# Pinning PSUM banks in an attention and two-layer MoE kernel: one bank for the first products of block 2, three for its attention

## The chip, the cores and the metric

The kernel runs on one NeuronCore of one Trainium2 chip. The metric is the device time of one execution in microseconds (us), the median of several. TensorE (PE) multiplies matrices and writes its results to PSUM, which has eight banks of 128 partitions by 2 KB. ScalarE (ACT) and VectorE (DVE) read them out of there, GpSimd (POOL) helps with element-wise work between tiles in SBUF, and SyncE (SP) issues most transfers.

## The reference

Three stages follow each other; the output of each is the input of the next.

```python
# q, k, v: (4, 8, 576, 64); omega: (128, 64)
def phi(x):                       # x already scaled by 64 ** -0.25
    h = x @ omega.T - sum(x * x, -1) / 2
    return exp(h - max(h, -1)) / sqrt(128)
q_p, k_p = phi(q_s), phi(k_s)
kv, z = k_p.T @ v, sum(k_p, axis=seq)
x = (q_p @ kv) / (q_p @ z + 1e-06)        # -> 2304 tokens x 512
h = x @ w_in                               # layer 1: 512 -> 2048
x = (h * clip(h + 3, 0, 6) / 6) @ w_out    # 2048 -> 512
h = x @ w_in2                              # layer 2: 512 -> 2048
x = (h * sigmoid(1.702 * h)) @ w_out2      # 2048 -> 512
```

## The kernel before, in words

**Stages.** The 4 x 576 = 2304 tokens are cut into four blocks of 512 (n = 0 to 3, one per batch) and a left-over block of 4 x 64 = 256 (i = B = 4). The attention of block 0 runs alone at the start (the head). Then layer one runs block by block. While layer one works on block n, the attention steps of block n + 1 are issued between its matmuls (`side()` takes them from the list `todo`), so block 2 carries the attention of block 3, the last one, and block 3 has no attention beside it but computes the left-over block as well. Layer two follows with a scheme of seven half-size products.

**Layer one** has 16 chunks c of 128 hidden columns per block. `emit_h` makes the first product of a chunk, `ps` (12 matmuls of 128x512, line 489: four pieces of the inner dimension, each as three products of a high and a low part). ACT applies relu (line 500), DVE the upper limit and the factor (line 501); only then is the bank of `ps` free. ACT and DVE split the result into two parts `gs` (lines 505, 506). `emit_o`, two chunks later (LAG = 2), multiplies `gs` with the second weights into `o` (line 531, 12 matmuls), which stays in its banks over all 16 chunks. In block 3 each chunk has these products twice, at 512 and at 256 columns.

**Attention steps** on PE are the projection with omega (line 265: pieces of 64 rows by 128), transposes of the features (line 345), k-features times v (lines 323, 331), q-features times that (lines 362, 371), and transposes of the normalised result (line 409, and 418 for the left-over rows). Their results leave PSUM through DVE (maximum, line 271; normalisation, lines 389, 393, 397) and ACT (exp, line 273; copy of `kv`, line 339; high part of x, line 255). Meanwhile ACT, DVE and POOL also prepare the weights of layer two (lines 189 to 229).

**PSUM.** Two pools of four banks. `acc` holds `o`. `psp` has one tag "ps" with four interchangeable banks: each request, from `emit_h` or from an attention step through `bank()`, takes whichever bank comes free.

```python
    acc = ctx.enter_context(tc.tile_pool(name="acc", bufs=4, space=PSUM))
    psp = ctx.enter_context(tc.tile_pool(name="psp", bufs=4, space=PSUM))
```

In block 3 the left-over block's `o` takes two banks of `psp` for the whole block. Layer two uses both pools.

**Order.** No order is written out by hand: a scheduler orders each engine's instructions by a timeline of its own, in which the banks that are free take part. So a change of the pools moves instructions on PE, ACT and DVE in all stages, also where the code of a stage is not touched. At run time each engine keeps its order.

Of the kernel before, what the change touches and what calls it, by code (L numbers as in the profile page):

```python
# [8 lines left out]
F32 = mybir.dt.float32  # L9
# [8 lines left out]
PSUM = bass.MemoryType.PSUM  # L18
# [4 lines left out]
def performer_moe_kernel(  # L23
# [18 lines left out]
    B, NPAIR, P = qk.shape[:3]  # L42
# [27 lines left out]
    wp = wctx.enter_context(tc.tile_pool(name="wp", bufs=1))  # L70
    dp = ctx.enter_context(tc.tile_pool(name="dp", bufs=1, space=DRAM))
    acc = ctx.enter_context(tc.tile_pool(name="acc", bufs=4, space=PSUM))
    psp = ctx.enter_context(tc.tile_pool(name="psp", bufs=4, space=PSUM))
    actx = ExitStack()
    at = actx.enter_context(tc.tile_pool(name="at", bufs=1, side="right"))

# [7 lines left out]
    banks = ["both"]  # L84

    def bank(shape, name):
        n_ps[0] += 1
        if banks[0] == "acc" or banks[0] == "both" and n_ps[0] % 2:
            return acc.tile(shape, F32, tag="acc", name="acc")
        return psp.tile(shape, F32, tag="ps", name="ps")  # L90

    def behind(*ins):
        stack = ExitStack()
# [386 lines left out]
    def emit_h(n, c, side):  # L480
        w = ws[0, "i", c].rearrange("p s (k f) -> p s k f", k=NK)
        for i, N in SEGS[n]:
            pool = lp if i == B else gp
            x = xblk[i]
            ps = psp.tile([P, N], F32, tag="ps", name="ps")
            m = 0
            for kk in range(NK):
                for wi, xi in ((0, 0), (0, 1), (1, 0)):
                    nc.tensor.matmul(  # L489
                        out=ps,  # L490
                        lhsT=w[:, wi, kk, :],
                        rhs=x[:, xi, kk, :],
                        start=(m == 0),
                        stop=(m == 3 * NK - 1),
                    )
                    m += 1
                if kk == 1:
                    side()
            g = pool.tile([P, N], F32, tag="ga", bufs=3, name="ga")
            nc.scalar.activation(out=g, in_=ps, func=AF.Relu, bias=three)  # L500
            nc.vector.scalar_tensor_tensor(  # L501
                out=g, in0=g, scalar=6.0, in1=ps, op0=ALU.min, op1=ALU.mult
            )
            s = pool.tile([P, 2, N], F32R, tag="gs", bufs=3, name="gs")
            gate[0] = nc.scalar.copy(s[:, 0, :], g)  # L505
            gate[1] = nc.vector.tensor_tensor(  # L506
                out=s[:, 1, :], in0=g, in1=s[:, 0, :].bitcast(F32), op=ALU.subtract
            )
            if i == n:
                late_at("next")  # L510
                late_at("gate")
            hgt[i, c] = s
            side()
# [3 lines left out]
    def emit_o(n, c, side):  # L517
        for i, N in SEGS[n]:
            w = ws[0, "o", c]
            s = hgt.pop((i, c))  # L520
            per = SM // N
            num = NK // per
            if c == 0:
                pool, tag = (psp, "ps") if i == B else (acc, "acc")
                oacc[i] = [pool.tile([P, per, SM // per], F32, tag=tag, name="o") for _ in range(num)]
            for d, ps in enumerate(oacc[i]):
                for e in range(per):
                    j = d * per + e
                    cols = slice(j * P, (j + 1) * P)
                    for m, (wi, gi) in enumerate(((0, 0), (1, 0), (0, 1))):  # L530
                        nc.tensor.matmul(  # L531
                            out=ps[:, e, :],
                            lhsT=w[:, wi, cols],
                            rhs=s[:, gi, :],
                            start=(c == 0 and m == 0 and e == 0),
                            stop=(c == NC - 1 and m == 2 and e == per - 1),
                            skip_group_check=per > 1,
                        )
                if c == NC - 1:
                    ob = evict(ps.rearrange("p e s -> p (e s)"), 1.0 / 6.0, n == B - 1)  # L540
                    nc.sync.dma_start(
                        out=xs[i][d * per:(d + 1) * per].rearrange("e p s -> p e s"),
                        in_=ob.rearrange("p (e s) -> p e s", e=per),
                    )
                if d == 1:
                    side()
            side()
# [112 lines left out]
    ps = bank([P, 4, P], "ps")  # L660
# [122 lines left out]
    for u in range(len(units) + LAG):  # L783
        while fetches and fetches[0][0] <= u + AHEAD:
            fetch_w(0, *fetches.pop(0)[1:])
        if u < len(units):
            n, c = units[u]
            if c == 0 and n + 1 < B:
                xblk[n + 1] = new_x(n + 1)
                steps = att_steps(Att(n + 1, xblk[n + 1], xl))  # L790
                todo = steps[::-1]
                pace[:] = len(todo), 0, 8 * (n > 0)
            if (n, c) == (B - 2, NC - 1):
                while todo:
                    todo.pop()()
                actx.close()
                lp = ctx.enter_context(
                    tc.tile_pool(name="lp", bufs=1, side="right", reuse_waits="tile")
                )
                xblk[B] = new_x(B)  # L800
                for kk in range(NK):
                    split_x(xl, xblk[B], kk)
            if n > 0:
                before_chunk(n, c)
            emit_h(n, c, side)
            if n == 0:
                convert_next(2, min(c + 2, NC), *(att.feat[H - 1] if c == 0 else ()))
            if (n, c) == (B - 1, PREP):
                assert n_late[0] == len(late)
                prep, _ = x_ops(0, wp, "w")  # L810
            if c == NC - 1:
                while todo:
                    todo.pop()()
        if u >= LAG:
            emit_o(*units[u - LAG], side)
# [5 lines left out]

    def h_pair(p, u, side, first_split):

        psum, tag, oth, otag = (acc, "acc", psp, "ps") if u % 2 else (psp, "ps", acc, "acc")
        w = {}

        def product(op, kind, j, ps, first):
# [88 lines left out]
        if last:  # L916
            rest(1, pl)
            if u % 2 == 0:
                pool, tag = ((l1, "xr"), (xp_, "xl"), (l1, "gl"), (l1, "xr"))[u // 2]
# [28 lines left out]
    def o_pair(p, side):  # L948
# [75 lines left out]
        def banks(pool, tag):  # L1024
            return [pool.tile([P, 2, H2], F32, tag=tag, name="o") for _ in range(2)]
# [15 lines left out]
        def left_bank(pool, tag):  # L1041
            return pool.tile([P, 2, H2], F32, tag=tag, name="o") if last else [None, None]
# [8 lines left out]
        if last:  # L1051
            tl = lp.tile([P, 4, H2], F32, tag="xo0", name="ob")
            tm = lp.tile([P, 4, H2], F32, tag="xo1", name="ob")
        l17 = left_bank(psp, "ps")
        o1 = banks(psp, "ps")
        product(1, o1, True, l17[:, 0] if last else None)
        if last:
            nc.scalar.copy(tl[:, 0], l17[:, 0])
# [4 lines left out]
        product(7, o7, True, l17[:, 1] if last else None)  # L1063
        if last:
            nc.scalar.copy(tl[:, 1], l17[:, 1])
        l6 = left_bank(psp, "ps")
        o6 = banks(acc, "acc")
        product(6, o6, True, l6[:, 0] if last else None)
        if last:
            add(tl[:, 2], tl[:, 0], l6[:, 0])  # L1070
        for j in range(2):
            add(u2[j], u2[j], o6[j])
        o5 = banks(psp, "ps")
        l5 = left_bank(acc, "acc")
        product(5, o5, True, l5[:, 0] if last else None)
        for j in range(2):
# [136 lines left out]
```

## Time and profile before

| | |
|---|---|
| median of 3 runs | 916.0 us (914.94 to 916.13) |
| the profiled execution's own time | 914.51 us |
| its span in the profile | 912.7 us, granted clock 0.998 |
| PE busy in the span | 896.9 us (98%) |
| DVE, ACT, POOL busy | 556.0, 477.4, 322.7 us |

The span runs from the first to the last instruction of the profile; 1.8 us of the execution lie around it. In the span, the head lasts to about 57 us, layer one's blocks 0 to 3 to about 173, 289, 410 and 548 us, and layer two to the end.

### The profile page before, as it was taken

The numbers are of one execution on the slowest core, as the hardware profiler recorded it, in microseconds if no ns is written. First come the engines' busy times: TensorE is split into PE (matmuls) and PEld (weight loads), VectorE is DVE, ScalarE is ACT, GpSimd is POOL, SyncE is SP. The second block draws the span as 40 slices with busy tenths as digits, with TensorE's granted clock in tenths as the row PEclk, the third lists the DMA queues.
The fourth block names the chain that finished last, engine by engine and source line by source line (L and its number), as shares of the span: only waits on it lengthen the run. The fifth ranks groups of instructions, "written<-read, shape, count | busy, mean of one in ns | idle before, by whom it ended". The sixth has DMA issues, their size and how long they took to land.

```text
span 912.7 us, 16524 instructions
## 1 busy us (share of the span) xinstructions
PE 896.9 (98%) x6344; PEld 764.8 (84%) x6344; DVE 556.0 (61%) x952; ACT 477.4 (52%) x973; POOL 322.7 (35%) x257
## 2 busy tenths in 40 slices
PE   8899999999999999999999999999999999999998
PEld 6677777788788788878888888778999888899998
DVE  5887787473744745558553343777876433367784
ACT  6888776376654765656542333444544232244442
POOL 0122222054736656374772112974000244330000
PEclk9999999999999999999999999999999999999999
DMA  7677678688888987778765436999889555465562
GB/s 227 224 252 271 216 268 299 250 308 269 306 284 296 351 303 291 251 268 288 278 227 188 152 121 234 369 398 307 274 293 326 204 165 181 161 174 152 141 199 78
DMA packets 74415, 224.57 MB, mean 246 GB/s; under 512 B 7520, under 2 KB 13792, under 8 KB 74336
## 3 DMA queue, kind: packets, MB, share of 16 engines
q1 hardware_dynamic: 73872, 223.12, 71.1%
q8 instruction: 50, 0.82, 0.4%
q10 hardware_dynamic: 464, 0.39, 0.1%
q14 instruction: 29, 0.24, 0.1%
HBM read 160.57 MB, written 62.91 MB: 245 GB/s over the span
## 4 chain that ended last, share of the span: by engine, by line
PE 84%; DVE 7%; ACT 6%; issue 1%; POOL 1%; DMA 0%; DVEq 0%; SPq 0%; ACTq 0%
PE o L976 20%; PE o L531 19%; PE ps L489 19%; PE h L832 15%; PE ps L265 3%; PE hl L849 2%; ACT e L273 2%; PE ps L362 1%; PE ps L323 1%; DVE w L212 1%; PE ps L345 1%; DVE mx L271 1%; ACT wtop L189 1%; DVE gs L506 1%; DVE wtop L197 1%
## 5 line engine op out<-in xcount | busy, mean ns | idle before, releaser
L489 PE MATMUL ps<-x,wss 128*128 128x512 f32 x768 | 194.6, 398 | 1.5 <-ACT wss L215 0.7
L976 PE MATMUL o<-wss,gs 128*128 128x256 f32 x1512 | 182.1, 283 | 0.1
L976 PEld LDWEIGHTS o<-wss,gs 128*128 128x128 f32 x1512 | 181.6, 191 | 0.8 <-DVE gs L945 0.5
L489 PEld LDWEIGHTS ps<-x,wss 128*128 128x128 f32 x768 | 140.4, 189 | 33.7 <-ACT wss L215 2.4
L832 PE MATMUL h<-xo,wss 128*128 128x512 f32 x672 | 160.2, 394 | 0.9 <-DVE t L865 0.9
L832 PEld LDWEIGHTS h<-xo,wss 128*128 128x128 f32 x672 | 124.1, 188 | 28.7 <-DVE t L865 1.7
L204 POOL TENSOR_TENSOR w<-w,wpow 128x1024 f32<-128x1024 f32 x32 | 69.3, 2164 | 202.9 <-DVE wpow L201 150.8
L501 DVE SCALAR_TENSOR_TENSOR ga<-ga,ps 128x512 f32<-128x512 f32 x80 | 50.1, 631 | 121.9 <-ACT ga L500 121.9
L873 POOL TENSOR_TENSOR g<-g,c 128x512 f32<-128x512 f32 x48 | 64.1, 1337 | 168.4 <-ACT g L872 168.1
L944 ACT CAST gs<-g 128x512 fp32r<-128x512 f32 x112 | 69.4, 621 | 87.1 <-PE o L976 80.7
L531 PE MATMUL o<-gs,wsh 128*128 128x512 f32 (+1 forms) x480 | 112.3, 378 | 1.2 <-ACT gs L505 1.0
L531 PE MATMUL o<-gs,wss 128*128 128x512 f32 (+1 forms) x480 | 109.9, 374 | 0.1
L229 POOL TENSOR_TENSOR wsn<-w,wsn 128x512 fp32r<-128x512 f32 x64 | 86.6, 1368 | 62.3 <-ACT wsn L228 58.2
L945 DVE TENSOR_TENSOR gs<-g,gs 128x512 fp32r<-128x512 f32 x112 | 79.9, 716 | 40.6 <-ACT gs L944 39.0
L531 PEld LDWEIGHTS o<-gs,wsh 128*128 128x128 f32 x480 | 82.2, 188 | 19.0 <-ACT gs L505 1.3
L500 ACT ACTIVATE ga<-ps,three 128x512 f32<-128x512 f32 x80 | 51.4, 650 | 89.2 <-PE ps L489 88.9
L531 PEld LDWEIGHTS o<-gs,wss 128*128 128x128 f32 x480 | 82.4, 188 | 16.2 <-ACT gs L505 0.3
L506 DVE TENSOR_TENSOR gs<-ga,gs 128x512 fp32r<-128x512 f32 x80 | 62.8, 795 | 16.6 <-ACT gs L505 14.7
L273 ACT ACTIVATE e<-ps,mx 128x128 f32<-128x128 f32 x220 | 60.9, 394 | 21.9 <-DVE mx L271 21.9
L872 ACT ACTIVATE g<-c 128x512 f32<-128x512 f32 x48 | 30.3, 632 | 61.5 <-DVE c L865 61.5
L505 ACT CAST gs<-ga 128x512 fp32r<-128x512 f32 x80 | 45.9, 579 | 27.5 <-DVE ga L501 27.1
L228 ACT CAST wsn<-w 128x512 fp32r<-128x512 f32 x64 | 38.2, 620 | 38.4 <-DVE w L212 13.3
(132 smaller groups left out, 1101.4 us busy)
## 6 DMA issues: line engine op xcount, KB each, us to landing
wss<-left SPq DMA_DIRECT2D x56, 512.0 KB, 3.8
wss<-ws0i SPq DMA_DIRECT2D x48, 512.0 KB, 4.7
wraw<-in_w_in_dram SPq DMA_DIRECT2D x32, 512.0 KB, 5.0
wraw<-in_w_out_dram SPq DMA_DIRECT2D x32, 512.0 KB, 6.2
left<-wsn SPq DMA_DIRECT2D x32, 512.0 KB, 3.9
wss<-ws0o SPq DMA_DIRECT2D x24, 512.0 KB, 4.7
ws0i<-wss SPq DMA_DIRECT2D x16, 512.0 KB, 3.1
wss<-sumsa SPq DMA_DIRECT2D x16, 512.0 KB, 3.8
```

The source lines that it names most:

```text
L204: nc.gpsimd.tensor_tensor(out=w, in0=w, in1=q, op=ALU.mult)
L229: nc.gpsimd.tensor_tensor(out=s[:, :, 1], in0=t, in1=s[:, :, 0].bitcast(F32), op=ALU.subtract)
L273: act = nc.scalar.activation(out=e[:, r, :], in_=ps[:, r, :], func=AF.Exp, bias=mx[:, r:r + 1])
L489: nc.tensor.matmul(out=ps, lhsT=w[:, wi, kk, :], rhs=x[:, xi, kk, :], start=(m == 0), stop=(m == 3 * NK - 1),)
L500: nc.scalar.activation(out=g, in_=ps, func=AF.Relu, bias=three)
L506: gate[1] = nc.vector.tensor_tensor(out=s[:, 1, :], in0=g, in1=s[:, 0, :].bitcast(F32), op=ALU.subtract)
L531: nc.tensor.matmul(out=ps[:, e, :], lhsT=w[:, wi, cols], rhs=s[:, gi, :], start=(c == 0 and m == 0 and e == 0), stop=(c == NC - 1 and m == ...
L832: nc.tensor.matmul(out=ps, lhsT=s[:, wi, q, :], rhs=xop[q, op][:, xi], start=(first and m == 0), stop=(m == 5), skip_group_check=not first,)
L873: mul = eng.tensor_tensor(out=g, in0=g, in1=src, op=ALU.mult)
L944: split_ins[0] = nc.scalar.copy(hi, g)
L945: split_ins[1] = nc.vector.tensor_tensor(out=lo, in0=g, in1=hi.bitcast(F32), op=ALU.subtract)
L976: last_row[0] = nc.tensor.matmul(out=out, lhsT=s[:, gi, d * P:(d + 1) * P], rhs=w[:, wi, :], start=(start and m == 0), stop=(stop and m == 2),
```

## The change

The pool `psp` is cut into two tags: "pa" with three banks and "ph" with one. A small class gives them out. In block 2 (`SPLIT[0]`, set for n == 2) the first products of layer one use "ph" alone and the attention steps "pa" alone. Everywhere else a request takes, in turn, pa, pa, pa, ph, by a count of the requests, so a request's tag is settled when the program is written, whichever bank is free. In block 3 the left-over block's `o` lies in two of the three "pa" banks; the products there take turns over the other "pa" bank (three of four) and "ph". In layer two the tags are written out, and the count starts anew at each pair.

```diff
-    psp = ctx.enter_context(tc.tile_pool(name="psp", bufs=4, space=PSUM))
+    pspp = ctx.enter_context(tc.tile_pool(name="psp", bufs=1, space=PSUM))
+
+    class Turns:
+
+        n = 0
+
+        def tile(self, shape, dtype, tag, name):
+            if tag == "ps":
+                Turns.n += 1
+                tag = "pa" if Turns.n % 4 else "ph"
+            return pspp.tile(shape, dtype, tag=tag, bufs=3 if tag == "pa" else 1, name=name)
+
+    psp = Turns()
+    SPLIT = [False]
...
-        return psp.tile(shape, F32, tag="ps", name="ps")
+        return psp.tile(shape, F32, tag="pa" if SPLIT[0] else "ps", name="ps")
...
-            ps = psp.tile([P, N], F32, tag="ps", name="ps")
+            ps = psp.tile([P, N], F32, tag="ps" if not SPLIT[0] else "ph" if i < B else "pa", name="ps")
...
-                pool, tag = (psp, "ps") if i == B else (acc, "acc")
+                pool, tag = (psp, "pa") if i == B else (acc, "acc")
...
             n, c = units[u]
+            SPLIT[0] = n == 2
...
-        psum, tag, oth, otag = (acc, "acc", psp, "ps") if u % 2 else (psp, "ps", acc, "acc")
+        psum, tag, oth, otag = (acc, "acc", psp, "pa") if u % 2 else (psp, "ps", acc, "acc")
+        Turns.n = 0
...
-        l17 = left_bank(psp, "ps")
-        o1 = banks(psp, "ps")
+        l17 = left_bank(psp, "ph")
+        o1 = banks(psp, "pa")
...
-        l6 = left_bank(psp, "ps")
+        l6 = left_bank(psp, "ph")
...
-        o5 = banks(psp, "ps")
+        o5 = [psp.tile([P, 2, H2], F32, tag=tag, name="o") for tag in ("pa", "ph")]
```

The added lines shift the later ones: lines 265, 323, 331, 345, 362, 371, 409, 418, 489 and 531 of before are lines 278, 336, 344, 358, 375, 384, 422, 431, 502 and 544 of the changed kernel.

**PE at the end of block 2's attention.** `x_3514` is block 3's input, `x_2194` block 2's. Before, in PE's order:

```order
L323 MATMUL ps<-v,e 64x65 x8
L331 MATMUL ps<-lv_94,el 64x65 x2
L531 MATMUL o<-gs,wss 128x512 x12
L362 MATMUL ps<-kv,qpt 64x65 x8
L371 MATMUL ps<-kv,qtl 64x65 x2
L531 MATMUL o<-gs,wss 128x512 x12
L409 MATMUL ps<-ident,xt 128x128 x4
L418 MATMUL ps<-ident,xln 64x64 x8
L489 MATMUL ps<-x_2194,wss 128x512 x12
L489 MATMUL ps<-x_3514,wss 128x512 x12
```

In the changed kernel, at the same place:

```order
L544 MATMUL o<-gs,wsh 128x512 x8
L336 MATMUL ps<-v,e 64x65 x8
L344 MATMUL ps<-lv_94,el 64x65 x2
L375 MATMUL ps<-kv,qpt 64x65 x8
L384 MATMUL ps<-kv,qtl 64x65 x2
L422 MATMUL ps<-ident,xt 128x128 x4
L431 MATMUL ps<-ident,xln 64x64 x8
L502 MATMUL ps<-x_3514,wss 128x512 x22
```

The last four attention steps, which had twelve matmuls of layer one between them twice, now follow each other directly, and block 2's last first product no longer stands behind them.

**PE at the start of block 2.** With the numbers of the tiles: `ps_3515`, `ps_3558` are the first products of chunks 0 and 1 of block 2, `ps_3656`, `ps_3657`, `ps_3728` belong to the attention. Before:

```order
L489 MATMUL ps_3515<-x2_2194,wss_3356 128x512 x9
L531 MATMUL o_2346<-gs_3378,wss_3354 128x512
L489 MATMUL ps_3558<-x2_2194,wss_3450 128x512 x9
L531 MATMUL o_2343<-gs_3472,wsh_2071 128x512
L489 MATMUL ps_3515<-x2_2194,wss_3356 128x512
L489 MATMUL ps_3558<-x2_2194,wss_3450 128x512
L531 MATMUL o_2343<-gs_3472,wsh_2071 128x512 x2
L489 MATMUL ps_3515<-x2_2194,wss_3356 128x512 x2
L489 MATMUL ps_3558<-x2_2194,wss_3450 128x512 x2
```

In the changed kernel, from the last part of chunk 0's product to chunk 1's:

```order
L502 MATMUL ps_3515<-x2_2194,wss_3356 128x512 x2
L278 MATMUL ps_3656<-omt_168,qk_3166 128x128
L278 MATMUL ps_3657<-omt_168,qk_3166 128x128
L278 MATMUL ps_3656<-omt_168,qk_3166 128x128
L278 MATMUL ps_3657<-omt_168,qk_3166 128x128
L278 MATMUL ps_3656<-omt_168,qk_3166 128x128
L278 MATMUL ps_3657<-omt_168,qk_3166 128x128
L278 MATMUL ps_3656<-omt_168,qk_3166 128x128
L278 MATMUL ps_3728<-omt_168,lqk_3170 128x128
L502 MATMUL ps_3558<-x2_2194,wss_3450 128x512 x12
```

Both products were open at once, in two banks; now the second starts only behind one group of projection matmuls, in the one bank that the first has used. Over the whole of block 2, stretches of small matmuls (lines 278, 336, 344, 375, 384, 431) in PE's order number 25, against 20 before; over block 1 19 and 19, over block 0 33 against 35.

**PE in block 3.** `x_3514` marks the products of 512 columns, `xl_4805` those of 256. Before, a piece of the middle of the block:

```order
L489 MATMUL ps<-x_3514,wss 128x512 x12
L489 MATMUL ps<-xl_4805,wss 128x256 x12
L531 MATMUL o<-gs,wsh 128x512 x12
L531 MATMUL o<-gs,wsh 128x256 x12
L489 MATMUL ps<-x_3514,wss 128x512 x12
L489 MATMUL ps<-xl_4805,wss 128x256 x12
```

In the changed kernel:

```order
L502 MATMUL ps<-x_3514,wss 128x512 x12
L544 MATMUL o<-gs,wsh 128x256 x2
L544 MATMUL o<-gs,wss 128x512 x12
L544 MATMUL o<-gs,wss 128x256 x12
L502 MATMUL ps<-xl_4805,wss 128x256 x3
L502 MATMUL ps<-x_3514,wss 128x512 x12
L502 MATMUL ps<-xl_4805,wss 128x256 x9
L544 MATMUL o<-gs,wsh 128x512 x12
```

The two first products of a chunk stood side by side; now they mostly have second products between them.

## Rows read from the trace of the kernel before

**Rows 1.** Busy time by engine in two stages: start to end, length, engines, clock, DMA.

```profile
0.00:57.00 57.00, 48.68 (x582) 37.68 (x582) 42.29 (x98) 41.35 (x115) 8.16 (x12) 0.97 0.71 234
...
289.00:410.00 121.00, 120.46 (x910) 96.13 (x907) 68.72 (x113) 74.88 (x169) 70.51 (x63) 1.00 0.83 294
```

**Rows 2.** PE's waits over the whole span: total, times, longest.

```profile
PE acc L362 <- ACT kv L339: 3.0, 3, 1.5
...
PE ps L409 <- DVE den L389: 1.1, 1, 1.1
```

**Rows 3.** PE's waits in block 2, from 289 to 410.

```profile
PE ps L489 <- ACT el L273: 0.4, 1, 0.4
```

**Rows 4.** The chain that ended last, in block 3: start, length, work.

```profile
451.55 4.17 PE o L531 x24
455.72 4.17 PE ps L489 x24
```

**Rows 5.** Timeline of PE around a long stretch of projections: start, length, work.

```profile
308.30 0.86 PE L531 MATMUL o<-gs,wsh 128*128 128x512 f32 x3
309.09 1.16 PE L265 MATMUL ps<-omt,lqk 64*128 64x128 f32 x16
310.18 1.42 PE L531 MATMUL o<-gs,wss 128*128 128x512 f32 x5
```

**Rows 6.** Timeline of PE around a short stretch of projections.

```profile
96.64 0.48 PE L265 MATMUL ps<-omt,qk 64*128 64x128 f32 x2
97.06 1.66 PE L531 MATMUL o<-gs,wsh 128*128 128x512 f32 x6
```

**Rows 7.** Timeline of PE at the end of block 2's attention.

```profile
399.85 3.04 PE L531 MATMUL o<-gs,wss 128*128 128x512 f32 x12
402.82 0.69 PE L362 MATMUL ps<-kv,qpt 128*64 128x65 f32 x16
403.33 0.29 PE L371 MATMUL ps<-kv,qtl 128*64 128x65 f32 x4
403.55 3.04 PE L531 MATMUL o<-gs,wss 128*128 128x512 f32 x12
406.42 0.60 PE L409 MATMUL ps<-ident,xt 128*128 128x128 f32 x4
```

**Rows 8.** Timeline of ACT, then DVE, at that place.

```profile
399.97 0.21 ACT L339 COPY kv<-ps 128x65 f32<-128x65 f32 x1 [0.52 <-PE ps L331]
...
403.67 0.17 DVE L389 TENSOR_SCALAR den<-ps 128x5 f32<-128x5 f32 x1 [2.12 <-PE ps L371]
...
404.09 0.42 DVE L397 TENSOR_TENSOR xt<-ps,rden 128x256 f32<-128x256 f32 x1
```

**Rows 9.** Timeline: one first product and the two reads that free its bank.

```profile
282.70 3.03 PE L489 MATMUL ps<-x,wss 128*128 128x512 f32 x12
...
285.76 0.69 ACT L500 ACTIVATE ga<-ps,three 128x512 f32<-128x512 f32 x1 [0.49 <-PE ps L489]
286.49 0.69 DVE L501 SCALAR_TENSOR_TENSOR ga<-ga,ps 128x512 f32<-128x512 f32 x1 [2.69 <-ACT ga L500]
```

**Rows 10.** Timeline of a first product in block 2 and what frees its bank.

```profile
303.98 2.89 PE L489 MATMUL ps<-x,wss 128*128 128x512 f32 x12
...
309.76 3.58 DVE L212 TENSOR_TENSOR w<-w,wtop 128x512 f32<-128x512 f32 x4
...
313.26 0.67 DVE L501 SCALAR_TENSOR_TENSOR ga<-ga,ps 128x512 f32<-128x512 f32 x1
```

**Rows 11.** Busy time in two slices of the head, columns as in group 1.

```profile
41.00:42.00 1.00, 0.39 (x12) 0.39 (x14) 1.00 (x3) 1.00 (x4) 0.81 (x1) 1.00 0.31 94
...
43.00:44.00 1.00, 1.00 (x17) 0.88 (x18) 0.63 (x2) 1.00 (x5) 0.33 (x1) 0.50 0.99 381
```

**Rows 12.** Timeline of a chunk's 512-column first product early in block 3, and its last read.

```profile
447.22 2.91 PE L489 MATMUL ps<-x,wss 128*128 128x512 f32 x12
...
454.63 1.01 DVE L501 SCALAR_TENSOR_TENSOR ga<-ga,ps 128x512 f32<-128x512 f32 x2
```

## The prediction

> **What bounds the kernel now.** I read the busy time by stage first. PE is busy 896.9 of 912.7 us, and in block 2, where the bank of its own is given, 120.46 of 121.00 us [rows 1]. The list of PE's waits for that block has one entry, 0.4 us, for an exp that empties an attention bank [rows 3]. So next to no wait for a bank is there to be removed in block 2: at most 0.5 us. What PE still has idle lies mostly in the head, 57.00 - 48.68 = 8.3 us of it [rows 1], of which 3.0 us wait for ACT's copy of `kv` and 1.1 us for the normalisation [rows 2]. There DVE and ACT are the busier: 1.00 us each in the slice where PE has 0.39 [rows 11]. The head's PE pauses also show in the clock: a slice right after that one has a granted clock of 0.50, half speed [rows 11].
>
> With PE busy everywhere, time is decided by how long PE's own stream takes: the matmuls at their bare rate, plus what each turn to another shape adds, plus new waits that a changed order opens. The bare rate is in the chain: 24 second products, then 24 first ones of block 3, each time 12 at 512 and 12 at 256 columns, take 4.17 us [rows 4]. With a 256-column matmul at half a 512-column one plus little, that is 0.231 us for 512 columns and 0.117 for 256.
>
> **What a turn to small matmuls costs.** The number of matmuls doesn't change; only into how many stretches the small ones are cut. Around a long stretch of 16 projections, three 512-column matmuls start at 308.30 and the projections at 309.09: 0.79 us, 0.10 more than 3 x 0.231. From the projections' start to the next large one are 1.09 us [rows 5]. A stretch of 2 takes 0.42 us by the same count [rows 6]. So one projection more costs (1.09 - 0.42) / 14 = 0.048 us; a stretch without any would take 0.42 - 2 x 0.048 = 0.32 us, and with the 0.10 of its entry its fixed part is **0.42 us**. That is what one stretch more costs; I let it go from 0.3 to 0.5. Block 2 has five stretches more: 5 x 0.42 = +2.1 us. Block 0 has two fewer: -0.8 us. Block 1 has as many as before. Sum **+1.3 us**, with bounds 0 (the extra stretches lie in waits that PE would have had anyway) and +2.5.
>
> **The end of block 2's attention.** Now twelve second products stand between the k-features' product and the q-features', and twelve more ahead of the transposes [rows 7]. They hide two reads. The copy of `kv` ends at 399.97 + 0.21 = 400.18, and PE was free for its reader at 399.85: 0.33 us, 0.4 with the hand-over. The normalisation ends at 404.09 + 0.42 = 404.51, and PE was free at 403.55: 0.96 us [rows 7, 8]; in the head, where nothing stands between them, PE waits 1.1 us for it [rows 2]. In the changed order the four steps touch, and both reads become waits: 0.4 + 1.1 = **+1.5 us**. Bounds: 0.9 (ACT and DVE come sooner because less stands in their queues) and 4 (an eviction or a weight conversion stands ahead of the copy; the conversion's four DVE instructions take 3.58 us [rows 10]). The transposes' own evictions stay covered by nine matmuls of block 3's first product, 2.1 us. What is late next is nothing: the 24 large matmuls that were cover are executed elsewhere in the block.
>
> **The start of block 2.** A first product's bank is free when DVE has read it: started at 282.70, its matmuls need 12 x 0.231 = 2.77 us, to 285.47, and DVE ends at 286.49 + 0.69 = 287.18, so 1.7 us later when neither engine is held up [rows 9]. In the changed order chunk 1's product follows chunk 0's in the same bank with one stretch of 16 projections between (the order's eight rows of pairs), 1.2 us [rows 5]. PE waits 1.7 - 1.2 = 0.5 us. Chunk 3's product waits about 0.65 us for exp and weight conversions in ACT's queue, by the same comparison, in place of the 0.4 us that chunk 2's attention costs now [rows 3]: +0.25. Together **+0.75 us**, bounds 0 and 5.5 (below). Behind such a wait on PE stand the second products, which are not urgent, and the projections, on whose maximum and exp DVE and ACT then run later.
>
> A rule of the Trainium skill speaks against this part of the change. What the row shows is that a freed bank comes 1.7 us after its matmuls [rows 9]. The page "Perfetto Trace Analysis", section "Optimizing Tensor Performance", says that independent groups of matmuls should go round several PSUM banks, so that the evacuation of one lies beside the next group's matmuls. By it, each of the 16 first products of block 2 would expose its 1.7 us, 27 us in all, and the time would be about 919.1 + 27 - 0.75 = 945. The order speaks against it, since second products and attention lie between most of them, and I give it 0.01, inside rival D.
>
> **The head and the other blocks.** Outside block 2 a request no longer takes the bank that is free first but the one that its turn names. By counting PE's time between two uses of a bank in the new order against 1.7 us, blocks 0 and 1 come to 0 (-0.4 to +0.8). In the head some projections now stand where PE waited for the normalisation, up to 1.1 us [rows 2]; since ACT and DVE are full there, I take half: **-0.5 us** (0 to -1.1). Block 3 has two banks for its first products in place of two interchangeable ones, and three of four fall on one. In its middle that bank always has at least one set of twelve large matmuls, 2.77 us, between two uses, against 1.7 us: **0** (to +8, below). Layer two's banks are the same in number and nothing there waits for `psp`: 0.
>
> **Sum.** 1.3 + 1.5 + 0.75 - 0.5 = +3.1 us. The profiled execution took 914.51 us, 1.5 under the median of 916.0; 914.5 + 3.1 = 917.6, on the median's scale **919.1 us**, +0.34%. A difference under 0.2% (1.8 us; 914.2 to 917.8) can't be told from none.
>
> **Rivals.** A, the forecast, 917.8 to 922: 0.43.
>
> B, no change, about 916.5: the extra stretches and the end's waits fall together. An instruction that waits at the end's reads or at the bank has its shape change behind the wait, and projections that are issued in a wait cost nothing. Then only 1.5 + 0.75 - 0.5 less what the pieces hide remain, or the pieces alone. For it: block 2's DVE and ACT are only 57% and 62% busy [rows 1], so evictions can be prompt. Against it: five stretches can't all lie in 2.25 us of waits that sit at two places. 0.26.
>
> C, faster, about 913.6: the head is reordered as a whole, and PE's idle time there shrinks. 8.3 us are idle [rows 1], 4.1 of them the waits for `kv` and the normalisation [rows 2], and without the longest pause the stretch at half speed, at least 1.0 us of loss in the two slices, would go too [rows 11]. It must give 3.6 + 1.8 = 5.4 us, all of that at once, to pass the mark; at 6 us the time is 919.1 + 0.5 - 6 = 913.6. Or the pieces and the end cost nothing and the head alone gives 2.3. Against it: where PE waits, DVE and ACT are full, and no work is taken from them. 0.19.
>
> D, much slower, over 922, about 926: late releases. In block 2 a product that ended at 306.75 had its bank freed at 313.26 + 0.67 = 313.93, 7.2 us later, because ACT's exps and DVE's 3.58 us of conversion stood ahead [rows 10]. With four banks nobody noticed. With one, a chunk of 121 / 16 = 7.6 us leaves 7.6 - 2.77 = 4.8 us between two first products; beyond 4.8 us each such release costs the difference, here 2.4 us. In block 3 one product, done at 449.99, was freed at 454.63 + 0.69 = 455.3, 5.3 us later [rows 12]; with 3.3 us of cover in the new order early in that block it costs 2.0. Two of each give +8.8 us less what lies in A: 926. Against it: the new order has DVE and ACT in another sequence, which was made with the one bank in view. 0.12.
>
> **How the numbers follow.** Slower by over 0.2%: A and D, 0.55. Within: B, 0.26. Faster: 0.19. The forecast's own range is 917.8 to 922. For 8 in 10 the range reaches down past B into C, to 913.3, and up into D, to 923.5; about 0.11 of C and 0.07 of D lie outside.
>
> **What would show it.** Block 2 longer by about 4 us, with PE's waits listing `kv` and the normalisation at its end (0.4 and 1.1 us) and first products waiting for DVE's read, the minimum and product of line 501 before, at its start; 25 stretches of small matmuls there; blocks 0, 1, 3 and layer two each within 1 us of before; the head shorter by about half a us. I am wrong if block 2 shows no new waits, if the head or layer two moves by more than 2 us, or if block 3's first products wait for their bank.

## The result and the profile after

The changed kernel takes 921.59 us (median of 4, 919.86 to 922.71), the kernel before 915.99: ratio 1.0062, 95% interval 1.005 to 1.0073. It is slower by 5.6 us where 3.1 were forecast; the time lies in the range given and in that of the forecast, 917.8 to 922. The profiled execution took 922.71 us, 8.2 more than that of before. It is the longest of the four, and that of before is 1.5 us under its median, so the sums by stage below are larger than the 5.6 us of the medians.

The same two stages that [rows 1] show, by the same clock times, and a slice early in block 3:

```profile
0.00:57.00 57.00, 47.44 (x586) 36.73 (x587) 42.57 (x100) 41.74 (x115) 8.15 (x12) 1.00 0.75 239
289.00:410.00 121.00, 119.93 (x829) 94.67 (x827) 68.90 (x107) 74.51 (x165) 71.60 (x61) 1.00 0.85 301
418.00:420.00 2.00, 2.00 (x5) 1.61 (x6) 0.69 (x1) 1.70 (x5) 1.10 (x2) 0.50 0.05 15
```

PE is as busy as it was, but in 289 to 410 it got through 829 matmuls where [rows 1] show 910: 76 small ones of the attention, which was over at 407.6 before, now come later, up to 418. And from 418 to 420 its granted clock is 0.50, the lower of its two levels (1.2 of 2.4 GHz). Before, the whole of that stretch ran at 1.00.

Where the time went is seen best when both executions are compared at equal work. For this I weighed every matmul of PE at its bare rate (0.231 us for 512 columns, 0.119 for 256, 0.06 for 128, 0.035 for the narrow ones) and took the difference of the times at which both had done the same sum. By stages, in us against before, with a second profile of the same kernel (experiment e10):

```
stage (before's clock time)            forecast   922.71 run   920.67 run
start to block 2 (to 285)                -1.3        -0.6         -0.2
block 2, body (285 to 399)               +2.0        +2.4         +2.2
end of its attention (399 to 422)        +2.3        +4.5         +2.5
rest of block 3 (422 to 554)              0          +1.0         +1.0
first part of layer two (554 to 657)      0          +1.0         +0.6
sum                                      +3.0        +8.2         +6.2
```

(The forecast's five stretches of small matmuls stand here with three in the body and two at the end, as the trace counts them.) From 657 us on, nothing changes.

In the first stage the head is 0.9 and 0.4 us shorter at 57 us, about as forecast, and block 1 0.8. But block 0, forecast 0.8 shorter, is 1.1 us longer in both runs. First products there wait for weights that ACT prepares (line 228): 2.5 us in three waits from 57 to 173, the longest 1.4 us at 160, where before it was 0.7 us in two.

PE's waits from 289 to 330, and then from 412 to 480:

```profile
PE ps L502 <- DVE ga L514: 1.0, 2, 0.6
```

```profile
PE ps L422 <- DVE xln L410: 1.9, 1, 1.9
PE ps L502 <- DVE ga L514: 1.2, 1, 1.2
PE ps L375 <- ACT kv L352: 0.3, 1, 0.3
```

In [rows 3] block 2 had one wait of 0.4 us. Now the first products of chunks 1 and 3 wait 0.4 and 0.6 us for their one bank; then come the copy of `kv` (line 352), the normalisation (line 410) and one first product in block 3. The end of block 2's attention, PE and then DVE, answering to [rows 7, 8]:

```profile
413.37 0.29 PE L344 MATMUL ps<-lv,el 128*64 128x65 f32 x4
413.97 0.69 PE L375 MATMUL ps<-kv,qpt 128*64 128x65 f32 x16 [0.31 <-ACT kv L352]
414.49 0.29 PE L384 MATMUL ps<-kv,qtl 128*64 128x65 f32 x4
416.71 0.63 PE L422 MATMUL ps<-ident,xt 128*128 128x128 f32 x4 [1.94 <-DVE xln L410]
...
417.91 6.39 PE L502 MATMUL ps<-x,wss 128*128 128x512 f32 x20
```

```profile
411.48 0.42 DVE L410 TENSOR_TENSOR xt<-ps,rden 128x256 f32<-128x256 f32 x1
415.12 0.69 DVE L574 TENSOR_SCALAR ob<-o 128x512 f32<-128x512 f32 x1 [3.22 <-DMA xs<-ob]
415.73 0.15 DVE L402 TENSOR_SCALAR den<-ps 128x5 f32<-128x5 f32 x1
415.92 0.19 DVE L406 RECIPROCAL rden<-den 128x5 f32<-128x5 f32 x1
416.14 0.42 DVE L410 TENSOR_TENSOR xt<-ps,rden 128x256 f32<-128x256 f32 x1
416.48 0.21 DVE L410 TENSOR_TENSOR xln<-ps,rden 128x64 f32<-128x64 f32 x1
```

Two things are to be seen. First, the four steps touch, as the order said, and PE pauses twice. Second, the pause ahead of the last transposes isn't the normalisation's own length. PE is through with its input at 414.8, but DVE begins at 415.73: ahead of it in DVE's queue stands an eviction of block 2's output (line 574), which has stood idle 3.22 us for a store that must free its buffer `ob`. Before, the attention ended ahead of block 2's output, so that no such eviction was there. And then the twenty large matmuls from 417.91, which at the bare rate take 20 x 0.231 = 4.6 us, take 6.4.

### The profile page after: what moved, and what is told of

It reads as the page before. It is cut to its first block, busy times and chain, and to the rows that moved or that the text cites. A ratio compares the mean times of both kernels' runs of the same rounds, so it can differ in the third digit from the quotient of the medians.

```text
span 920.9 us, 16509 instructions
## 1 busy us (share of the span) xinstructions
PE 898.3 (98%) x6344; PEld 764.7 (83%) x6344; DVE 557.9 (61%) x952; ACT 478.2 (52%) x973; POOL 321.4 (35%) x257
## 4 chain that ended last, share of the span: by engine, by line
PE 76%; DVE 6%; ACT 6%; DMA 5%; POOL 5%; issue 3%; SPq 0%; DVEq 0%; POOLq 0%; ACTq 0%
PE o L991 19%; PE ps L502 17%; PE o L544 17%; PE h L847 12%; PE ps L278 3%; PE hl L864 2%; DMA xr<-xs 2%; ACT e L286 2%; PE ps L375 1%; DMA xs<-ob 1%; DMA qk<-in_qk_dram 1%; POOL wsn L242 1%; PE ps L336 1%; PE ps L358 1%; ACT wtop L202 1%
## 5 line engine op out<-in xcount | busy, mean ns | idle before, releaser
L514 DVE SCALAR_TENSOR_TENSOR ga<-ga,ps 128x512 f32<-128x512 f32 (+1 forms) x80 | 49.9, 633 | 124.6 <-ACT ga L513 124.3
L513 ACT ACTIVATE ga<-ps,three 128x512 f32<-128x512 f32 (+1 forms) x80 | 51.0, 651 | 96.5 <-PE ps L502 96.2
L519 DVE TENSOR_TENSOR gs<-ga,gs 128x512 fp32r<-128x512 f32 (+1 forms) x80 | 64.0, 805 | 25.8 <-ACT gs L518 24.5
L518 ACT CAST gs<-ga 128x512 fp32r<-128x512 f32 (+1 forms) x80 | 46.1, 579 | 39.0 <-DVE ga L514 38.3
L225 DVE TENSOR_TENSOR w<-w,wtop 128x512 f32<-128x512 f32 x64 | 47.5, 789 | 14.2 <-POOL w L217 14.2
```

Source lines behind the costliest of these rows:

```text
L519: gate[1] = nc.vector.tensor_tensor(out=s[:, 1, :], in0=g, in1=s[:, 0, :].bitcast(F32), op=ALU.subtract)
```

## The experiments

Theory A, held from here on: the split makes the loss in block 2, most of it at the end of the attention. Its rivals: pinned banks outside block 2 (B), the single bank and the cut stretches all over the body (B2), the dependency alone without DVE's queue (C). The letters of the experiments are these, not those of the prediction's cases.

**e1: pinned banks, no split.**

```diff
-            SPLIT[0] = n == 2
+            SPLIT[0] = False
```

> The changed kernel with block 2 not split: there too the requests take pa, pa, pa, ph in turn. In the order of PE the last normalisation of block 2's attention has 12 first and 9 second products behind it again before its transposes. Theory A (the loss is made in block 2 by the bank of its own and lies mostly at the end of its attention, where PE pauses and then runs at half clock): no half-clock stretch at the start of block 3, the shift there below 1.5 us; what is left is about -0.6 from the head, +1.2 from the shared bank of block 3 and +0.8 at the start of layer two, so 916 to 918.5. Rival B (the loss comes from pinned banks outside block 2, where before any free bank would do): 920.5 to 922.5, as the changed kernel.

919.05 us (6 runs), ratio 1.0044 (1.0029 to 1.006): half a microsecond above A's range, lower than B's. The end of block 2 costs 0.1 us here, as A had it, and the profiled run shows another loss, 7.9 us in the body of block 2. That run, 923.06, is the longest of the six; the other five took 918.5 to 919.7, so they can't have had all of it. DVE, PE, and the clock there:

```profile
311.95 3.57 DVE L225 TENSOR_TENSOR w<-w,wtop 128x512 f32<-128x512 f32 x4
315.45 0.67 DVE L514 SCALAR_TENSOR_TENSOR ga<-ga,ps 128x512 f32<-128x512 f32 x1
```

```profile
316.18 1.16 PE L278 MATMUL ps<-omt,qk 64*128 64x128 f32 x16 [1.49 <-DVE ga L514]
318.44 5.49 PE L502 MATMUL ps<-x,wss 128*128 128x512 f32 x12 [1.10 <-ACT el L286]
```

```profile
318.00:320.00 2.00, 1.56 (x4) 1.27 (x5) 1.21 (x3) 1.84 (x7) 1.92 (x3) 0.50 1.07 358
320.00:322.00 2.00, 2.00 (x6) 1.54 (x5) 0.00 (x0) 2.00 (x9) 1.92 (x3) 0.50 0.96 380
```

This is the late release of [rows 10], now with a price: a projection is assigned to the bank of a first product whose second read stands behind 3.57 us of weight conversion, waits 1.49 us, the next first product 1.10, and PE then runs at half clock. At 357.65 PE waits another 2.21 us, for a normalisation, and a second stretch at 0.50 follows. So pinning has a cost of its own, at another place: by the medians 919.05 - 915.64 = 3.4 us without any split. Taking the split out of the changed kernel therefore gives back only 2.5 of its 5.6 us.

**e2: split in block 2, interchangeable banks elsewhere.** The pool is opened anew at the two ends of block 2.

```diff
...
-            if tag == "ps":
-                Turns.n += 1
-                tag = "pa" if Turns.n % 4 else "ph"
-            return pspp.tile(shape, dtype, tag=tag, bufs=3 if tag == "pa" else 1, name=name)
+            if not cut[1]:
+                return cut[2].tile(shape, dtype, tag="ps", bufs=4, name=name)
+            return cut[2].tile(shape, dtype, tag=tag, bufs=3 if tag == "pa" else 1, name=name)
...
             SPLIT[0] = n == 2
+            if c == 0 and n > 1:
+                open_psp(n == 2)
```

> Four interchangeable banks before and after block 2, as in the kernel before; the split into three and one only in block 2 (the pool is closed and opened anew at its two ends). PE's order is that of before up to block 2; the last four attention steps touch each other as in the changed kernel. Theory A: the loss of block 2 is all there, about +2.3 in its body and +4 at its end, so 920.5 to 923. Rival B: 915 to 917.

922.28 us, ratio 1.0077 (1.0062 to 1.0091), in A's range: the split alone, without pinned banks elsewhere, makes the whole loss and more, so B isn't needed for it. The two causes don't add up: 3.4 us for pinning alone, 6.6 for the split alone, 5.6 for both. By equal work the body costs 1.4 us, the end 5.1, the rest of block 3 1.7. PE's waits from 412 to 424 and the clock behind them:

```profile
PE ps L432 <- DVE xln L420: 2.4, 1, 2.4
PE ps L385 <- ACT kv L362: 0.3, 1, 0.3
```

```profile
418.00:420.00 2.00, 2.00 (x9) 1.52 (x6) 0.65 (x1) 1.70 (x5) 0.91 (x2) 0.50 0.04 15
```

**e3: a third output buffer.**

```diff
-            ob = gp.tile([P, SM], F32, tag="ob", bufs=2, name="ob")
+            ob = gp.tile([P, SM], F32, tag="ob", bufs=3, name="ob")
```

(and the same number where layer two uses the tag).

> The changed kernel with three output buffers ob in place of two. The last four attention steps still touch. Theory A with DVE's queue as the cause of the long pause (the normalisation stands behind an output eviction that waits for a buffer's store): the last transposes wait about 1.1 us in place of 2.2, and with the shorter pause no half-clock stretch of 4 us follows: 3 us less, about 918.5. Rival C (the pause is that of the dependency itself, whatever stands in DVE's queue): the clock falls as before, 921 to 922.

920.83 us, ratio 1.0057 (1.0045 to 1.0069). The total is nearer to C than to A, but the place says otherwise. PE's waits there and the clock:

```profile
PE ps L422 <- DVE xln L410: 1.0, 1, 1.0
PE ps L375 <- ACT kv L352: 0.3, 1, 0.3
```

```profile
418.00:420.00 2.00, 2.00 (x23) 1.67 (x20) 0.69 (x1) 1.93 (x6) 0.59 (x1) 1.00 0.33 125
```

With a buffer free, the pause is 1.0 us, near the 0.96 worked out from [rows 7, 8]: what made it longer was the eviction in DVE's queue. The clock holds, and the end costs 2.1 us in place of 4.5. How much of that the buffer gives is open: in e10 below the changed kernel itself keeps its clock and its end costs 2.5, so the buffer is sure for 0.4 us, and one profiled execution can't tell whether it also keeps the clock up. The edit moved the order in the body of block 2 too, which costs 3.2 here against 2.4, so the total shows only part of it.

**e4: the end's order in the kernel before.** Second products of chunks 13 to 15 of block 2 are ordered behind the attention's last matmul.

```diff
...
-                        nc.tensor.matmul(
...
+                        with behind(done[0] if n == 2 and c >= 13 and m == 0 else None):
+                            nc.tensor.matmul(
...
```

> The kernel before, with four interchangeable banks, in which second products of chunks 13 to 15 of block 2 are ordered behind the last transposes of its attention, so that the last steps of it touch each other on PE; up to there the order is that of before. Theory A: waits of 0.4 and 1.1 us, so +1.5 (917.5) if the clock holds, +3.5 (919.5) if the pause takes it down. Rival B: within 1 us of before, 915 to 917.

916.81 us (11 runs), ratio 1.0014 (1.0006 to 1.0023). PE:

```profile
401.18 0.69 PE L364 MATMUL ps<-kv,qpt 128*64 128x65 f32 x16 [0.31 <-ACT kv L341]
401.70 0.29 PE L373 MATMUL ps<-kv,qtl 128*64 128x65 f32 x4
403.30 0.66 PE L411 MATMUL ps<-ident,xt 128*128 128x128 f32 x4 [1.32 <-DVE xt L399]
```

0.31 and 1.32 us, the two waits of the forecast (0.4 and 1.1), with no change of banks at all; the clock holds and the end costs 1.8 us by equal work. That is the price of this order alone. The total, 1.2 us above the kernel before, lies in rival B's range and 0.7 under A's; by equal work block 3 gives 0.5 of the 1.8 back. So it is the waits, not the total, that bear A out.

**e5: as e2, split in chunks 0 to 11 only.**

Against e2:

```diff
-            SPLIT[0] = n == 2
-            if c == 0 and n > 1:
-                open_psp(n == 2)
+            SPLIT[0] = n == 2 and c < 12
+            if (n, c) in ((2, 0), (2, 12)):
+                open_psp(c == 0)
```

> As the kernel with the split in block 2 alone and four interchangeable banks elsewhere, but with the split only in chunks 0 to 11 of block 2. The last steps of the attention have twelve second products between them again, in the order of the kernel before. Theory A (of the 6.6 us that the split in block 2 alone cost, the end of the attention makes about 5, by PE's pause and the half clock behind it, and the cut stretches and the single bank in the body 1 to 2): 916.5 to 918. Rival B2 (the single bank and the cut stretches themselves make most of it, all over the block): 920 to 922.

917.62 us (10 runs), ratio 1.0024 (1.0015 to 1.0033). PE at the end, with the second products between again:

```profile
406.48 0.29 PE L394 MATMUL ps<-kv,qtl 128*64 128x65 f32 x4
406.69 3.04 PE L554 MATMUL o<-gs,wss 128*128 128x512 f32 x12
409.56 0.60 PE L432 MATMUL ps<-ident,xt 128*128 128x128 f32 x4
```

By equal work the end costs 0.0 us, the body 2.2, and what follows nothing; the part up to block 2 is 1.0 us longer in this execution. Against e2 the difference of the medians is 922.28 - 917.62 = 4.7 us. In the two profiles the end makes 5.1 of it and the rest of block 3 1.7, less 1.9 by which e5 is longer up to and in the body. B2, which had 920 to 922, is out.

**e6: the changed kernel, split in chunks 0 to 11 only.**

```diff
-            SPLIT[0] = n == 2
+            SPLIT[0] = n == 2 and c < 12
```

> The changed kernel, pinned banks elsewhere included, with the split only in chunks 0 to 11 of block 2; twelve first products of chunk 15 stand between the last normalisation and the last transposes. Theory A: no half clock at the start of block 3 and no wait for the normalisation over 0.5 us: 4 us less than the changed kernel's profile, 917 to 919. Rival B2: 920.5 to 922.5.

918.19 us, ratio 1.0028 (1.0017 to 1.0039), 3.4 under the changed kernel. No wait is listed from 405 to 430, and the clock holds; the end costs 0.5 us, the body 3.8, and block 3, with its banks pinned as in the changed kernel, -0.3.

**e7: the changed kernel, split in chunks 12 to 15 only.**

```diff
-            SPLIT[0] = n == 2
+            SPLIT[0] = n == 2 and c >= 12
```

> The changed kernel with the split only in chunks 12 to 15 of block 2. The last k-features' product has 21 second products behind it, the last normalisation five (1.2 us). Theory A: the wait for the normalisation is 0 to 0.3 us if DVE is not held by an output eviction, and no half clock at the end; the body is that of the kernel without split, which cost 3.4 us with all its parts: 918 to 920. Rival B2 (the body of the split makes the loss): the same. Rival D (any split at the end brings the pause): 921 to 923.

922.26 us, ratio 1.0071 (1.0059 to 1.0082): a miss for A. The body, pinned without split, costs 5.2 us, with a stretch at half clock in it behind this wait of 2.22 us, the same as the second one in e1:

```profile
348.43 2.89 PE L544 MATMUL o<-gs,wss 128*128 128x512 f32 x12
353.54 1.08 PE L422 MATMUL ps<-ident,xt 128*128 128x128 f32 x4 [2.22 <-DVE xln L410]
```

It says that the split's end isn't the only place at which such a pause can fall: a pinned body can have it too. The rest of block 3 and the start of layer two cost 1.5 us each. But the end costs only 0.3, as A had it, though the attention ends as late as in the changed kernel:

```profile
413.63 1.80 PE L544 MATMUL o<-gs,wsh 128*128 128x512 f32 x7
415.36 0.69 PE L375 MATMUL ps<-kv,qpt 128*64 128x65 f32 x16
416.09 1.44 PE L544 MATMUL o<-gs,wsh 128*128 128x512 f32 x5
417.36 0.60 PE L422 MATMUL ps<-ident,xt 128*128 128x128 f32 x4
```

There are still second products between the steps, and PE waits at neither read. That speaks against rival D, though the total lies in its range.

**e8: two interchangeable banks for block 3's first products.**

```diff
-            ps = psp.tile([P, N], F32, tag="ps" if not SPLIT[0] else "ph" if i < B else "pa", name="ps")
+            ps = psp.tile([P, N], F32, tag="pa" if n == B - 1 else "ph" if SPLIT[0] else "ps", name="ps")
...
-                pool, tag = (psp, "pa") if i == B else (acc, "acc")
-                oacc[i] = [pool.tile([P, per, SM // per], F32, tag=tag, name="o") for _ in range(num)]
+                pool, tags = (psp, ("pa", "ph")) if i == B else (acc, ("acc",) * num)
+                oacc[i] = [pool.tile([P, per, SM // per], F32, tag=tag, name="o") for tag in tags]
```

> The changed kernel with one edit in block 3: the left-over block's second products take one pa bank and ph, so that the first products have two interchangeable pa banks, as in the kernel before. The order up to block 3 is that of the changed kernel. Theory A: the wait of 1.2 us for DVE in the middle of block 3 goes, the rest stays: 920.0 to 921.0. If the shared bank makes a larger part of the loss than the one wait, 918 to 919.5.

Median 921.99 us, ratio 1.0071 (1.0058 to 1.0084), neither of the two. Its runs fall apart: 921.66, 921.99, 922.20, 922.45, and the profiled one 918.43. In that one DVE's eviction waited 2.58 us for the store and PE 1.29 for the normalisation, and the clock held:

```profile
413.93 0.69 DVE L574 TENSOR_SCALAR ob<-o 128x512 f32<-128x512 f32 x1 [2.58 <-DMA xs<-ob]
```

```profile
415.52 0.63 PE L422 MATMUL ps<-ident,xt 128*128 128x128 f32 x4 [1.29 <-DVE xln L410]
```

The long wait in the middle of block 3 is gone (two short ones of 0.35 and 0.23 us are left), but the rest of block 3 costs 1.3 us all the same. The shared bank thus isn't shown as its cause. All this is of the fastest execution; what made the other four 3.2 to 4.0 us longer, no profile shows.

**e9: block 2's last first product held back.** In the changed kernel it is issued behind the last k-features' product of the attention, to serve as cover.

```diff
...
-                    nc.tensor.matmul(
...
+                    with behind(done[0] if (n, c) == (2, NC - 1) and m == 0 else None):
+                        nc.tensor.matmul(
...
```

> The changed kernel, with the split and all pinned banks, with one order more: the first product of block 2's last chunk is issued behind the last k-features' product of the attention. PE's order is that of the changed kernel up to the last 20 us of block 2; then twelve first products stand between the k-features' and the q-features' product and eight second products ahead of the last transposes. Theory A (the end of block 2 costs so much because the first products, with a bank of their own, have run out before the attention ends): no waits over 0.3 us there, full clock, the end within 0.7 us of before, the total 2.5 to 4.5 us under the changed kernel, 917 to 919. If the loss isn't bound to this cover, 920.5 to 922.5.

922.21 us, ratio 1.0069 (1.0056 to 1.0081): a miss. The attention's waits went and the clock holds, but others came. PE's waits from 405 to 560, and one place:

```profile
PE ps L505 <- DVE ga L517: 2.4, 3, 1.3
PE o L547 <- ACT gs L521: 1.4, 1, 1.4
PE o L547 <- DVE gs L522: 0.6, 1, 0.6
```

```profile
411.68 0.29 PE L386 MATMUL ps<-kv,qtl 128*64 128x65 f32 x4
413.39 2.13 PE L547 MATMUL o<-gs,wsh 128*128 128x512 f32 x8 [1.42 <-ACT gs L521]
```

The second products that were to follow wait for the split result of the very product that was held back. The end costs 2.4 us, the rest of block 3 3.3. So the place of twelve matmuls alone doesn't help where what follows them isn't ready. Counted in the traces, the large matmuls of block 2 still to come when its attention ends are 24 before, 0 in the changed kernel, in e2, e3 and e8, 4 here, and 12 and 24 in e6 and e5, where the end costs next to nothing. But e7 has 0 as well, and its end costs 0.3 us: what counts is the large matmuls between the steps, not those left behind them.

**e10: the changed kernel once more.**

> The changed kernel, once more, to see its end of block 2 in another execution. Theory A: either the pause ahead of the last transposes is near 2 us, half clock follows and the run takes 922 to 923, or it is near 1.3 us, the clock holds and the run takes 919.5 to 920.5. If the clock doesn't follow the pause, the two are mixed.

920.67 us, one run. PE, and the slice that stood at 0.50 above:

```profile
414.80 0.29 PE L384 MATMUL ps<-kv,qtl 128*64 128x65 f32 x4
416.59 0.63 PE L422 MATMUL ps<-ident,xt 128*128 128x128 f32 x4 [1.50 <-DVE xln L410]
```

```profile
418.00:420.00 2.00, 2.00 (x10) 1.62 (x10) 0.57 (x1) 1.58 (x5) 1.24 (x2) 1.00 0.02 6
```

The same program, DVE's eviction held 2.79 us by the store in place of 3.22, full clock, and 2.04 us less in all. By equal work the difference lies at this place, 4.5 against 2.5 (0.4 more at the start and 0.4 less in layer two cancel). So about 0.4 us of it is the longer pause and 1.6 the clock. The wait, 1.50 us, is between the two that the expectation named, and the time just above its lower range.

That the longer pause brought the lower clock isn't shown by this. In the head of the same two executions PE waits equally long for `kv`, and the clock differs. PE, in the changed kernel's first profile and then in e10:

```profile
40.48 0.69 PE L375 MATMUL acc<-kv,qpt 128*64 128x65 f32 x16 [2.85 <-ACT kv L352]
...
40.92 1.13 PE L375 MATMUL acc<-kv,qpt 128*64 128x65 f32 x16 [2.85 <-ACT kv L352]
```

The slice from 42 to 44, in the same order:

```profile
42.00:44.00 2.00, 1.64 (x21) 0.83 (x15) 1.77 (x4) 0.31 (x2) 0.00 (x0) 1.00 0.73 247
...
42.00:44.00 2.00, 2.00 (x24) 1.67 (x24) 1.67 (x5) 0.64 (x2) 0.20 (x1) 0.50 0.74 184
```

## Why the prediction was right, and where its sizes were off

The direction and the range held, and so did the main place: block 2's body and the end of its attention. The size didn't: 5.6 us for 3.1. The end is 2.2 us over its term in the 922.71 us run and nearly right in the 920.67 us run. In both, the first stage is over by 0.7 and 1.1 us, block 3 by 1.0 and layer two by 1.0 and 0.6, and these the forecast had at a gain or at nothing. That the time lies inside all the same is owed to the width of the range, and in part to luck.

**What bounds the kernel.** That there was no wait for a bank to remove in block 2 held. The prediction's rival C, the head, gave 0.2 to 0.6 us by the start of block 2, not 5.4: the wait of 1.1 us for the normalisation went, but the longest one for `kv` grew from 1.5 to 2.85. In the first profile the head kept its clock, as C had it, and still gained no more. For the whole stage -1.3 was forecast; what failed is block 0, where longer waits for weights from ACT ate up the 0.8 us of its two fewer stretches and more. Rival B, no change, would have needed the stretches to lie inside waits; the body shows both side by side.

**Stretches and the single bank.** 2.0 us were forecast for the body of block 2 and 2.2 to 2.4 measured. The waits for the one bank came at the two products named, with 0.41 and 0.59 us for 0.5 and 0.65. What is left, 2.36 less the 0.51 by which PE's waits there grew, is 1.85 us for three more stretches, 0.6 each and not 0.42; in e2, by the same reckoning, it is 0.63 for two, in e5 1.5 for four, and in e6 2.8 for five. The size per stretch is so known to 0.3 to 0.6. That the body's total came near its forecast is in part two misses that cancel: the waits grew by less than the 0.75 worked out, and the stretches cost more. The rule of the Trainium skill ("Perfetto Trace Analysis", section "Optimizing Tensor Performance") that groups should go round several banks names a real cost, but 1.0 us at two of sixteen products: with other work between two groups, one bank was nearly enough here.

**The end of the attention.** This is the term that was mis-sized, 4.5 us in the first profile for 2.3 with its two stretches. Its mechanism, the two reads that lose their cover, was right, and where nothing else happens its size nearly too: 1.8 us in e4, whose forecast was 1.5, and 2.1 with the two stretches in e3. What the working left out is what stands ahead of the read in DVE's queue: its input was there at 414.8, but it began at 415.73, because the attention, now late, ends among the evictions of block 2's output. I had allowed for a weight conversion ahead of the read, not for an instruction that itself waits for a store: the pause is 1.3 to 2.4 us with it (the changed kernel, e2, e8, e10) and 1.0 without (e3). And I took a pause on PE to cost its length. At the end of block 2 a stretch at 0.50 followed where the listed wait was 1.9 and 2.4 us (the changed kernel's first profile, e2), and none where it was 1.0 to 1.5 (e3, e4, e8, e10). The length of the wait alone doesn't settle it: in the head the same 2.85 us had both outcomes, in e1 1.49 and 1.10 us close together were followed by 0.50, and in e7 a wait of 1.77 us in block 3 was not.

**Why the steps touch** was read from the order but not worked out: with a bank of its own, layer one runs ahead, and when the attention ends there are 0 and not 24 large matmuls left. Splitting only chunks 0 to 11 recovers 3.4 us (e6), or 4.7 with interchangeable banks elsewhere (e5 against e2). But e7, split only in chunks 12 to 15, pays nothing at the end either: neither part of the split brings the steps together, only both do. Being late isn't enough, since e7's attention ends at 418 with no large matmul left; it is the missing cover between the steps that costs. That the order makes this cover vanish because layer one has run ahead agrees with the counts, but wasn't varied by itself.

**Block 3 and layer two.** Forecast 0, measured 1.0 each in the first profile. The prediction had named a first product of block 3 that waits for its bank as a sign of being wrong, and one does. The wait of 1.2 us for DVE stands behind 3.57 us of weight conversion, as the prediction's rival D had it, and at equal work the stage's loss falls around it: 1.8 us between 440 and 475, less 0.8 gained in the rest of block 3. One such wait of 1.2 to 1.8 us stands in the middle of block 3 in e3, e7, e9 and e10 too, and in e2 behind other steps of the weights' preparation. These lose 1.0 us or more there; e5 and e6 have no such wait and lose nothing. As e2 has interchangeable banks and e6 pinned ones, it isn't the shared bank alone; e6 even has the same conversion ahead of the same read, without a wait. What brings them together, the 1.3 us of e8, and the 0.6 to 1.0 us at the start of layer two stay open. Such a late release was also seen in e1, in a kernel without the split.

None of these versions is faster than the kernel before; of those with a split, e5 is the nearest, at 917.6.

## What to carry to other kernels

A bank of its own for one of two interleaved streams doesn't only cost waits for that bank; it changes which stream gets ahead, and the one that falls behind can end with nothing between its steps to hide its reads. When a chain of steps loses its cover, look on every engine of the chain at what is ahead of it in the queue, above all at instructions that wait for a transfer. A pause on PE is then to be priced with both clocks: its length, and its length plus half of the time at the lower level that may follow.

## What the hardware showed unexpectedly

One pause of about 2 us in a stream that is 99% busy, with one of 0.3 us shortly ahead of it, was followed by a stretch at the lower granted clock: in the changed kernel 0.50 from 418 to 420 and a mean of 0.70 from 420 to 422, worth 1.6 us. Whether it comes differs between executions of one program: it makes 1.6 of the 2.0 us between the two profiled runs of the changed kernel. The five runs of that kernel fall into 919.9 to 920.7 and 922.6 to 922.7 us, which would fit with the stretch in two of them, but only two were profiled. What decides isn't known: at this place the pause was 0.4 us longer where the clock fell, while in the head a wait of 2.85 us in both runs was followed by 0.50 in one and 1.00 in the other. There it hardly mattered: at 57 us the two runs are 0.4 us apart. The Trainium skill's page "TensorE: Matmul & The Clock Gate", section "A second HAM failure mode: psum-queue depth-cycling", tells of PE losing throughput to such changes of the clock when it pauses between groups again and again; here the clock fell once, behind these two pauses.
